# Low parts of both layers' activations: from VectorE to GpSimd

## The chip, the cores and the metric

The kernel runs on one core of a Trainium2 chip. The metric is the device time of one execution in microseconds (us). The core has TensorE (PE, matmuls), VectorE (DVE), ScalarE (ACT), GpSimd (POOL) and SyncE (SP), which here issues the DMAs. Each works through its own queue in order, and they wait for each other by semaphores. TensorE's granted clock was 1.00 of full in nearly every stretch of the profile.

## What is computed

Attention in two stages over packed keys, then two dense layers, all in fp32:

```
x = attention(q, k, v, p)                  # 2304 tokens x 512
h = x @ moe_w_in;  g = softplus(h);  x = g @ moe_w_out      # 512 -> 2048 -> 512
h = x @ moe2_w_in; g = silu(h);      y = g @ moe2_w_out     # 512 -> 2048 -> 512
```

The weights arrive as 64-bit floats.

## The kernel before

Every operand of the large matmuls is kept as two fp32r tiles: a high part, which ScalarE makes by a copy with rounding, and a low part, the operand less its high part, which VectorE makes by a subtraction. A product is then three matmuls: low times high, high times low, high times high.

The **first layer** goes in steps. A unit is a block of 288 tokens (`N0`) and four tiles of 128 hidden features (`GJ`); each step does one tile. `emit_in` (line 484) computes h by 6 matmuls. `emit_out` (line 524) does 12 matmuls of the unit before into a product bank y. `act_scalar` makes the softplus `gt` (line 496, pool of two buffers) and the high part `gh` (line 497) on ScalarE; `act_vector` makes the low part `gl` (line 501). `finish_out` (lines 537 to 541) then adds y to `ya`, which frees the bank. The low part of a unit's last tile is wanted soonest: by the eleventh of the twelve output matmuls in the step right after it. Between these the steps carry out planned items, namely attention (its `ax` is the first layer's input) and the conversion of weights from 64 bits (`wx`, `wraw`, `w` for this layer, `wf`, `whl`, `ohl` for the next). They stand at fixed points of a step; the order on each engine is the order of the code, since the schedule is made by hand.

The **second layer** goes in 24 steps (`step`) of 2 x 384 tokens and 2 x 128 hidden features. It makes a two by two block product of seven products Q1 to Q7 (`products`, line 837) into the banks pA to pD, and sums of them on VectorE (`tu`, `tc`, `c`, by the helper `add`, line 887). Then come silu and high part on ScalarE (lines 907, 908 for g11; 934, 935 for c12; 938, 939 for the pair c2) and three low parts on VectorE into halves of `G` (also through `add`, so the trace gives them line 887). Between the products stand the output tiles of earlier steps (`out_tile`, line 853, 12 matmuls each), and their addition to `ya` (line 866). An even step reads the first token half, also that of the step just before; an odd one reads the second half of two and three steps before. At step 6 the next tokens' operand `xc` is split: high on ScalarE (line 565), low on VectorE (line 569). Its memory was that of the converted weights `whl`, which must first have been stored to `wd`.

GpSimd does a few memsets and the identity matrix at the start, and nothing later.

Of the kernel before, what the change touches and what calls it, by code (L numbers as in the profile page):

```python
# [8 lines left out]
F32 = mybir.dt.float32  # L9
# [4 lines left out]
ALU = mybir.AluOpType  # L14
# [33 lines left out]
def body(ctx, tc, kT, vv, qT, pT, wi1, wo1, wi2, wo2, out):  # L48
    nc = tc.nc
# [130 lines left out]
    def close_stage():  # L180
        stage_stack.close()
        stage_stack.__init__()
# [315 lines left out]
        return gt, gh, gl  # L498

    def act_vector(s, gt, gh, gl):  # L500
        nc.vector.tensor_tensor(out=gl, in0=gt, in1=gh.bitcast(F32), op=ALU.subtract)  # L501
        gs[steps[s]] = gh, gl

    def emit_out(s):
# [223 lines left out]
    def run_steps(end):  # L728
        for s in range(end):
# [21 lines left out]
            if r:  # L751
                act_vector(s, *r)
# [19 lines left out]
    def load_i1(t):  # L772
        if t < NSLOT and (2 * t + 1) // NQ % NJ not in stored:
            held.append(t)
        elif t < NSLOT:
            w = ring_i[t] = wp.tile([P, 2 * DM], F32R, name="w", tag=f"i{t % RI}")
            c = t % (NJ * NQ // 2) * 2 * DM
            nc.sync.dma_start(out=w.bitcast(F32), in_=wd[:, c:c + 2 * DM])
# [39 lines left out]
    def second():  # L818
        psa_stack.close()
        pb = pool("pb", 1, space=PSUM)  # L820
        tmp = st["tmp"]
        slots = [*range(6)]
        G = None
        gs1, frees = {}, {}
        count, put_off = [0], []

        def bank():
            count[0] += 1
            return ps.tile([P, 512], F32, name="y", tag="hy"[count[0] % 2])[:, :N1]

        def products(k, q, out, start):
            p = k * NQ + q
            w = ring_i[p // 2][:, p % 2 * DM:p % 2 * DM + DM]
            x = xcs[k // NJ % 2]
            mm = [(w[:, i * NW + kt * P:i * NW + (kt + 1) * P], x[:, q, h, kt]) for i, h in ((1, 0), (0, 1), (0, 0)) for kt in range(2)]
            for i, (a, b) in enumerate(mm):
                nc.tensor.matmul(  # L837
                    out, lhsT=a, rhs=b, start=start and not i, stop=not start and i == len(mm) - 1,
                    skip_group_check=True,
                )  # L840
            if p % 2:
                load_i1(p // 2 + RI)

        def out_tile(f, t, dm):
            y = bank()
            c = slice(dm * P, (dm + 1) * P)
            for k in 2 * f, 2 * f + 1:
                g = gs1[k, t]
                for j in range(2):
                    w = ring_o[2 * k + j]  # L850
                    wh, wl = w[:, :DM], w[:, DM:]
                    for m, (a, h) in enumerate(((wl, 0), (wh, 1), (wh, 0))):
                        nc.tensor.matmul(  # L853
                            y, lhsT=a[:, c], rhs=G[:, g, h, j], start=(k % 2 == j == m == 0),
                            stop=(k % 2 == j == 1 and m == 2),
                        )
            return y

        def add_out(f, t, dm, y):
            s, f = divmod(f, NPASS)  # L860
            c = (2 * s + t) * N1
            acc = ya[:, dm, c:c + N1]
            if not f:
                nc.scalar.activation(out=acc, in_=y, func=AF.Copy)
            else:
                nc.vector.tensor_tensor(out=acc, in0=y, in1=acc, op=ALU.add)  # L866
            if f == NPASS - 1:
                nc.sync.dma_start(out=out[dm * P:(dm + 1) * P, c:c + N1], in_=acc)

        def out_of(k, i):  # L870
            if not k:
                (dm, y), = emit_out(NS + i)
                return lambda: finish_out(NS + i, dm, y)
            f, t = divmod(k - 2, 2)
            if f < 0:
                return lambda: None
            y = out_tile(f, t, i)
            return lambda: add_out(f, t, i, y)

        def step(k):  # L880
            nonlocal G
            go = lambda p: [fn() for fn in fills.get((k, p), ())]
            y = {}
            b = {n: pb.tile([P, 512], F32, name=f"p{n}")[:, :N1] for n in "ABCD"}
            t = {n: tmp.tile([P, N1], F32, name=f"t{n}") for n in ("a", "u2", "u3", "g11", "c12")}
            c2 = tmp.tile([P, 2, N1], F32, name="c2")
            add = lambda o, i, j, op=ALU.add: nc.vector.tensor_tensor(out=o, in0=i, in1=j, op=op)  # L887
            late = k in (1, 2)
            go("L")
            products(k, Q1, b["A"], True)  # L890
            nc.scalar.activation(out=t["a"], in_=b["A"], func=AF.Copy)  # L891
            products(k, Q6, b["B"], True)
            add(t["u2"], t["a"], b["B"])
            if put_off:
                put_off.pop()()
            go("A0")
            go("D0")
            if not late:
                y[0] = out_of(k, 0)
            products(k, Q2, b["A"], False)  # L900
            products(k, Q7, b["B"], False)
            if late:
                y[0] = out_of(k, 0)
            if G is None:
                G = big.tile([P, 6, 2, 2, N1], F32R, name="G", tag="A")
            g1 = gs1[k, 0] = slots.pop(0)
            nc.scalar.activation(out=t["g11"], in_=b["A"], func=AF.Silu)  # L907
            nc.scalar.activation(out=G[:, g1, 0, 0], in_=t["g11"], func=AF.Copy)
            if not late:
                y.pop(0)()  # L910
            add(t["u3"], t["a"], b["B"])
            add(G[:, g1, 1, 0], t["g11"], G[:, g1, 0, 0].bitcast(F32), ALU.subtract)
            if late:
                y.pop(0)()
            go("D1")
            go("A1")
            go("M")
            y1 = out_of(k, 1)
            y1()
            products(k, Q5, b["C"], True)  # L920
            add(c2[:, 1], t["u3"], b["C"])
            go("D2")
            y2 = out_of(k, 2)
            y2()
            go("A2")
            if k == 1:
                products(k, Q4, b["D"], True)
                products(k, Q3, b["C"], False)
            else:
                products(k, Q3, b["C"], False)  # L930
                products(k, Q4, b["D"], True)
            def first_half():
                add(t["c12"], t["u2"], b["C"])
                nc.scalar.activation(out=t["c12"], in_=t["c12"], func=AF.Silu)  # L934
                nc.scalar.activation(out=G[:, g1, 0, 1], in_=t["c12"], func=AF.Copy)

            def second_half():
                nc.scalar.activation(out=c2, in_=c2, func=AF.Silu)
                nc.scalar.activation(out=G[:, g2, 0], in_=c2, func=AF.Copy)
                add(G[:, g2, 1], c2, G[:, g2, 0].bitcast(F32), ALU.subtract)  # L940

            if k == 1:
                add(c2[:, 0], t["u3"], b["D"], ALU.subtract)
                first_half()
            else:
                first_half()
                add(c2[:, 0], t["u3"], b["D"], ALU.subtract)
            add(G[:, g1, 1, 1], t["c12"], G[:, g1, 0, 1].bitcast(F32), ALU.subtract)
            y3 = out_of(k, 3)
            go("S")  # L950
            while held and (2 * held[0] + 1) // NQ % NJ in stored:
                load_i1(held.pop(0))
            y3()
            for i in frees.pop(k, ()):
                slots.append(i)
            g2 = gs1[k, 1] = slots.pop(0)
            if k == 1:
                put_off.append(second_half)
            else:
                second_half()  # L960
            go("A3")
            go("D3")
            for i, g in (0, g1), (1, g2):
                frees.setdefault(k // 2 * 2 + 2 + i, []).append(g)
            m = (k + 1) // 2 * GJ + (2 - k % 2 * 2)
            for i in range(2):
                if GJ <= m + i < NSUP * NF:
                    load_o1(m + i)
            if k == 0:
                l0_stack.close()  # L970
                open_stage(1, side="right", reuse_waits="tile")

        plan_second()
        for k in range(NSTEP):
            if k == 6:
                close_stage()
                open_xc(1, side="right", reuse_waits="tile")
            step(k)
        for k in NSTEP, NSTEP + 1:
            for i in range(KT):  # L980
                out_of(k, i)()
# [56 lines left out]
```

## Time and profile before

| | us |
|---|---|
| median of 3 runs | 757.52 |
| range of the runs | 756.37 to 760.15 |
| the profiled execution | 756.34 |
| its span (first to last instruction) | 754.6 |
| TensorE busy in it | 745.1 |
| VectorE busy | 494.3 |
| ScalarE busy | 364.7 |
| GpSimd busy | 0.7 |

The busy time of TensorE is modelled at its ends: matmuls overlap, so a row's length (0.29 us for 288 columns) is longer than the distance to the next (0.13 us). What TensorE loses to a wait is read from the distance of starts. "Idle before" is the time in which an engine had nothing to do, with what ended it. Idle time of an engine that TensorE does not wait for costs nothing.

### The profile page before, as it was taken

How to read it: one execution, taken by the hardware profiler on the slowest of the kernel's cores; microseconds unless marked ns; L12 is line 12 of the kernel's file. 1: busy time of each engine (PE TensorE's matmuls, PEld its weight loads, DVE VectorE, ACT ScalarE, POOL GpSimd, SP SyncE). 2: the span in 40 equal slices, each digit the busy share in tenths (PEclk: the TensorE clock that was granted, in tenths of full speed). 3: DMA queues.
4: the chain of work that ended last, by engine and by line, in shares of the span. 5: the costliest groups of instructions: out<-in, count | busy, mean ns of one | idle time of the engine just before them, and what ended most of it. 6: DMA issues, size and time to landing. Idle time of an engine off the chain costs nothing.

```text
span 754.6 us, 13458 instructions
## 1 busy us (share of the span) xinstructions
PE 745.1 (99%) x5488; PEld 713.3 (95%) x5488; DVE 494.3 (66%) x921; ACT 364.7 (48%) x684; POOL 0.7 (0%) x6
## 2 busy tenths in 40 slices
PE   8999999999999999999999999999999999999998
PEld 7777889999999999999999999999999999999998
DVE  3888887879877997897557775743343764334442
ACT  4677786656555565665445553422333323332230
POOL 0000000000000000000000000000000000000000
PEclk9999999999999999999999999999999999999999
DMA  9955032146444452566268888666565557655602
GB/s 343 342 212 183 2 140 113 56 182 197 185 151 182 140 195 86 201 246 267 62 230 336 345 299 325 229 216 204 174 220 193 167 189 238 231 180 168 223 0 85
DMA packets 38974, 145.92 MB, mean 193 GB/s; under 512 B 4352, under 2 KB 7936, under 8 KB 37376
## 3 DMA queue, kind: packets, MB, share of 16 engines
q1 hardware_dynamic: 38912, 145.06, 54.3%
q8 instruction: 43, 0.70, 0.4%
q14 instruction: 19, 0.16, 0.1%
HBM read 117.25 MB, written 27.79 MB: 192 GB/s over the span
## 4 chain that ended last, share of the span: by engine, by line
PE 89%; ACT 4%; DVE 3%; DMA 3%; issue 1%; SPq 1%; ACTq 0%
PE y L853 25%; PE y L524 24%; PE h L484 12%; PE pC L837 6%; PE pA L837 6%; PE pB L837 6%; PE pD L837 3%; PE psa L450 2%; PE y L517 2%; DMA wd<-whl 1%; DMA wraw<-wo 1%; PE psa L357 1%; ACT L419 0%; PE psa L405 0%; ACT ax L431 0%
## 5 line engine op out<-in xcount | busy, mean ns | idle before, releaser
L853 PE MATMUL y<-G,w 128*128 128x384 f32 x1152 | 213.7, 334 | 0.0
L524 PE MATMUL y<-gh,w 128*128 128x288 f32 x960 | 212.1, 296 | 0.3 <-DVE ya L539 0.2
L853 PEld LDWEIGHTS y<-G,w 128*128 128x128 f32 x1152 | 201.0, 188 | 0.0
L524 PEld LDWEIGHTS y<-gh,w 128*128 128x128 f32 x960 | 160.4, 188 | 13.0 <-issue 5.5
L524 PE MATMUL y<-gl,w 128*128 128x288 f32 x480 | 141.8, 295 | 0.1
L484 PE MATMUL h<-ax,vw 128*128 128x288 f32 x768 | 125.0, 298 | 0.3 <-DVE ax L433 0.3
L484 PEld LDWEIGHTS h<-ax,vw 128*128 128x128 f32 x768 | 109.3, 188 | 2.4 <-DVE ax L433 0.5
L524 PEld LDWEIGHTS y<-gl,w 128*128 128x128 f32 x480 | 90.2, 188 | 0.5 <-DVE gl L501 0.5
L866 DVE TENSOR_TENSOR ya<-y,ya 128x384 f32<-128x384 f32 x72 | 40.1, 557 | 64.9 <-PE y L853 64.6
L496 ACT ACTIVATE gt<-h 128x288 f32<-128x288 f32 x120 | 48.6, 405 | 68.6 <-PE h L484 63.9
L501 DVE TENSOR_TENSOR gl<-gt,gh 128x288 fp32r<-128x288 f32 x120 | 54.2, 452 | 25.1 <-ACT gh L497 24.3
L934 ACT ACTIVATE tc<-tc 128x384 f32<-128x384 f32 x24 | 12.6, 526 | 107.0 <-DVE tc L887 107.0
L837 PE MATMUL pC<-xc,w 128*128 128x384 f32 x288 | 57.8, 334 | 0.8 <-DVE c L887 0.8
L887 DVE TENSOR_TENSOR tu<-ta,pB 128x384 f32<-128x384 f32 x48 | 26.5, 552 | 48.4 <-PE pB L837 48.2
L837 PE MATMUL pA<-xc,w 128*128 128x384 f32 x288 | 57.8, 334 | 0.1
L837 PE MATMUL pB<-xc,w 128*128 128x384 f32 x288 | 57.7, 334 | 0.0
L497 ACT ACTIVATE gh<-gt 128x288 fp32r<-128x288 f32 x120 | 53.4, 445 | 3.8
L541 DVE TENSOR_TENSOR ya<-y,ya 128x288 f32<-128x288 f32 x104 | 46.9, 452 | 7.2 <-PE y L524 7.0
L837 PEld LDWEIGHTS pC<-xc,w 128*128 128x128 f32 x288 | 50.5, 188 | 1.1 <-DVE c L887 1.1
L837 PEld LDWEIGHTS pA<-xc,w 128*128 128x128 f32 x288 | 50.5, 188 | 0.4 <-ACT ta L891 0.4
L837 PEld LDWEIGHTS pB<-xc,w 128*128 128x128 f32 x288 | 50.6, 188 | 0.0
L907 ACT ACTIVATE tg<-pA 128x384 f32<-128x384 f32 x24 | 11.8, 491 | 58.2 <-PE pA L837 58.2
(90 smaller groups left out, 793.3 us busy)
## 6 DMA issues: line engine op xcount, KB each, us to landing
w<-wd SPq DMA_DIRECT2D x84, 512.0 KB, 4.0
w<-od SPq DMA_DIRECT2D x48, 512.0 KB, 5.3
wd<-whl SPq DMA_DIRECT2D x8, 1792.0 KB, 7.3
wraw<-wi SPq DMA_DIRECT2D x16, 512.0 KB, 5.5
wraw<-wo SPq DMA_DIRECT2D x16, 512.0 KB, 6.3
raw<-wi SPq DMA_DIRECT2D x16, 512.0 KB, 6.4
raw<-wo SPq DMA_DIRECT2D x16, 512.0 KB, 7.1
od<-ohl SPq DMA_DIRECT2D x16, 512.0 KB, 3.2
```

What stands on the lines that cost most here:

```text
L450: nc.tensor.matmul(t[32 * k:32 * k + 32, r, :512 if wide else 256], lhsT=pts[b][rows, k * NP:(k + 1) * NP], rhs=w[rows, :], start=True, st ...
L484: nc.tensor.matmul(h, lhsT=w, rhs=x, start=(i == 0), stop=(i == len(mm) - 1))
L496: nc.scalar.activation(out=gt, in_=h, func=AF.Softplus)
L497: nc.scalar.activation(out=gh, in_=gt, func=AF.Copy)
L501: nc.vector.tensor_tensor(out=gl, in0=gt, in1=gh.bitcast(F32), op=ALU.subtract)
L517: nc.tensor.matmul(y, lhsT=wo_plain[j][:, c], rhs=gs[u - 1, x], start=(j == js[0]), stop=(j == js[-1]))
L524: nc.tensor.matmul(y, lhsT=w[:, c], rhs=g, start=(j == js[0] and m == 0), stop=(j == js[-1] and m == 2))
L541: nc.vector.tensor_tensor(out=acc, in0=y, in1=acc, op=ALU.add)
L837: nc.tensor.matmul(out, lhsT=a, rhs=b, start=start and not i, stop=not start and i == len(mm) - 1, skip_group_check=True,)
L853: nc.tensor.matmul(y, lhsT=a[:, c], rhs=G[:, g, h, j], start=(k % 2 == j == m == 0), stop=(k % 2 == j == 1 and m == 2),)
L866: nc.vector.tensor_tensor(out=acc, in0=y, in1=acc, op=ALU.add)
L887: add = lambda o, i, j, op=ALU.add: nc.vector.tensor_tensor(out=o, in0=i, in1=j, op=op)
```

## The change

The subtractions that make the low part of the activations are issued to GpSimd. This concerns one line of the first layer (120 instructions of 128x288) and three of the second (24 each, two of 128x384 and one of 128x768). The low parts of weights, of attention's output and of the second layer's input stay on VectorE. So do all sums.

```diff
     def act_vector(s, gt, gh, gl):
-        nc.vector.tensor_tensor(out=gl, in0=gt, in1=gh.bitcast(F32), op=ALU.subtract)
+        nc.gpsimd.tensor_tensor(out=gl, in0=gt, in1=gh.bitcast(F32), op=ALU.subtract)
         gs[steps[s]] = gh, gl
...
             add = lambda o, i, j, op=ALU.add: nc.vector.tensor_tensor(out=o, in0=i, in1=j, op=op)
+            low = lambda o, x, h: nc.gpsimd.tensor_tensor(out=o, in0=x, in1=h.bitcast(F32), op=ALU.subtract)
...
-            add(G[:, g1, 1, 0], t["g11"], G[:, g1, 0, 0].bitcast(F32), ALU.subtract)
+            low(G[:, g1, 1, 0], t["g11"], G[:, g1, 0, 0])
...
-                add(G[:, g2, 1], c2, G[:, g2, 0].bitcast(F32), ALU.subtract)
+                low(G[:, g2, 1], c2, G[:, g2, 0])
...
-            add(G[:, g1, 1, 1], t["c12"], G[:, g1, 0, 1].bitcast(F32), ALU.subtract)
+            low(G[:, g1, 1, 1], t["c12"], G[:, g1, 0, 1])
```

VectorE's queue in the first layer, at the step of 177 us, where a weight tile of `w_out` is converted (lines 148 to 155, and its low part in line 169). Before:

```order
L148 TENSOR_SCALAR wx<-wraw 128x512 [waits DMAHW1_49]
L150 SCALAR_TENSOR_TENSOR wx<-wraw,wx 128x512 [waits DVE_49,Activation_49]
L155 SCALAR_TENSOR_TENSOR wx<-wraw,wx 128x512 [waits DVE_49]
L501 TENSOR_TENSOR gl<-gt,gh 128x288 [waits Activation_49]
L541 TENSOR_TENSOR ya<-y,ya 128x288 [waits PE_49]
L169 TENSOR_TENSOR w<-wx,w 128x512 [waits Activation_49]
L501 TENSOR_TENSOR gl<-gt,gh 128x288 [waits Activation_49]
L541 TENSOR_TENSOR ya<-y,ya 128x288 [waits PE_49]
```

And after, at the same place:

```order
L148 TENSOR_SCALAR wx<-wraw 128x512 [waits DMAHW1_49]
L150 SCALAR_TENSOR_TENSOR wx<-wraw,wx 128x512 [waits DVE_49,Activation_49]
L155 SCALAR_TENSOR_TENSOR wx<-wraw,wx 128x512 [waits DVE_49]
L541 TENSOR_TENSOR ya<-y,ya 128x288 [waits PE_49]
L169 TENSOR_TENSOR w<-wx,w 128x512 [waits Activation_49]
L541 TENSOR_TENSOR ya<-y,ya 128x288 [waits PE_49]
```

Two low parts are gone from this queue, and the additions behind them follow on the conversion. On TensorE the matmul that reads such a low part first waits for GpSimd (`Pool`) where it waited for VectorE, or for nothing of its own, before.

VectorE's queue in the second layer, at step 6 (454 to 466 us), from the sums of the first products to the end of the split of `xc`. Before:

```order
L887 TENSOR_TENSOR tu_5812<-ta,pB 128x384 [waits PE_49]
L887 TENSOR_TENSOR G<-tg_5813,G 128x384 [waits Activation_49]
L569 TENSOR_TENSOR xc_5805<-ya,xc_5805 128x768 [waits DMAHW7_49]
L866 TENSOR_TENSOR ya<-y,ya 128x384 [waits PE_49]
L887 TENSOR_TENSOR c_5815<-tu_5812,pC 128x384 [waits DVE_49,PE_49]
```

After:

```order
L887 TENSOR_TENSOR tu_5812<-ta,pB 128x384 [waits DVE_49,PE_49]
L569 TENSOR_TENSOR xc_5805<-ya,xc_5805 128x768 [waits DMAHW7_49,Activation_49]
L866 TENSOR_TENSOR ya<-y,ya 128x384 [waits PE_49]
L887 TENSOR_TENSOR c_5815<-tu_5812,pC 128x384 [waits DVE_49,PE_49,Pool_49]
```

The low part of `tg` no longer stands ahead of the split. The sum into `c` has a new wait for GpSimd, which reads the former content of `c` in the step before.

## Rows read from the trace of the kernel before

**Rows 1.** The page: span, and busy time, share and instructions by engine.

```profile
span 754.6 us, 13458 instructions
PE 745.1 (99%) x5488; PEld 713.3 (95%) x5488; DVE 494.3 (66%) x921; ACT 364.7 (48%) x684; POOL 0.7 (0%) x6
```

**Rows 2.** Stretches: length, busy us (instructions) by engine, clock, DMA share, GB/s.

```profile
40.00:80.00 40.00, 39.59 (x455) 30.92 (x453) 35.63 (x69) 30.06 (x55) 0.00 (x0) 1.00 0.47 164
80.00:160.00 80.00, 78.84 (x716) 73.93 (x716) 64.36 (x128) 55.17 (x113) 0.00 (x0) 1.00 0.29 108
160.00:240.00 80.00, 79.97 (x632) 75.72 (x632) 66.83 (x134) 47.10 (x99) 0.00 (x0) 1.00 0.46 162
500.00:600.00 100.00, 100.00 (x579) 100.00 (x578) 43.62 (x73) 33.58 (x58) 0.00 (x0) 1.00 0.61 201
```

**Rows 3.** Chain that ended last: start us, us on the chain, what.

```profile
371.11 1.58 PE y L524 x12
...
467.30 2.08 PE y L853 x12
```

**Rows 4.** Groups by line and shape: busy us, mean ns, idle before, releaser.

```profile
L887 DVE TENSOR_TENSOR G<-c,G 128x768 fp32r<-128x768 f32 x24 | 22.8, 952 | 19.3 <-ACT G L939 19.3
...
L887 DVE TENSOR_TENSOR G<-tc,G 128x384 fp32r<-128x384 f32 x24 | 13.4, 558 | 4.2 <-ACT G L935 1.8
...
L887 DVE TENSOR_TENSOR G<-tg,G 128x384 fp32r<-128x384 f32 x24 | 13.2, 551 | 3.0 <-ACT G L908 3.0
```

**Rows 5.** Tile gl: ns min/median/max, first and last start; who waited (us, times).

```profile
L501 DVE TENSOR_TENSOR gl<-gt,gh x120: 416/452/461, 58.5 to 368.4; 128x288 fp32r<-128x288 f32 x120
...
  PEld y L524: 0.9, 3
```

**Rows 6.** Groups by line, GpSimd alone: two of its six instructions.

```profile
masks.py:199 POOL TENSOR_SCALAR_AFFINE_SELECT ident<-ident 128x128 f32<-128x128 f32 x1 | 0.3, 294 | 0.1
...
L1031 POOL MEMSET const-float32-0.0<- 128x1 f32 x1 | 0.1, 99 | 0.2 <-issue 0.2
```

**Rows 7.** Timeline, end of an ordinary unit: start us, us, engine, line, what.

```profile
206.76 0.44 ACT L497 ACTIVATE gh<-gt 128x288 fp32r<-128x288 f32 x1
...
209.81 0.30 PE L524 MATMUL y<-gl,w 128*128 128x288 f32 x1
```

**Rows 8.** Timeline, unit end with a weight conversion before it.

```profile
176.57 0.45 ACT L497 ACTIVATE gh<-gt 128x288 fp32r<-128x288 f32 x1
...
177.57 0.69 DVE L155 SCALAR_TENSOR_TENSOR wx<-wraw,wx 128x512 int32<-128x512 int32 x1
...
178.18 0.45 DVE L501 TENSOR_TENSOR gl<-gt,gh 128x288 fp32r<-128x288 f32 x1
178.23 0.43 PE L524 MATMUL y<-gh,w 128*128 128x288 f32 x2
...
178.69 0.40 PE L524 MATMUL y<-gl,w 128*128 128x288 f32 x1
```

**Rows 9.** Timeline, second layer, step 6.

```profile
459.99 1.58 ACT L565 ACTIVATE xc<-ya 128x768 fp32r<-128x768 f32 x2 [5.72 <-DMA wd<-whl]
...
461.91 2.25 PE L853 MATMUL y<-G,w 128*128 128x384 f32 x12
...
462.54 0.56 DVE L887 TENSOR_TENSOR G<-tg,G 128x384 fp32r<-128x384 f32 x1 [3.00 <-ACT G L908]
463.02 0.95 DVE L569 TENSOR_TENSOR xc<-ya,xc 128x768 fp32r<-128x768 f32 x1
...
464.35 0.55 DVE L887 TENSOR_TENSOR c<-tu,pC 128x384 f32<-128x384 f32 x1
...
464.95 1.31 PE L837 MATMUL pC<-xc,w 128*128 128x384 f32 x6 [0.80 <-DVE c L887]
```

**Rows 10.** Timeline, end of the last step.

```profile
732.34 18.88 PE L853 MATMUL y<-G,w 128*128 128x384 f32 x108
...
732.65 0.53 ACT L935 ACTIVATE G<-tc 128x384 fp32r<-128x384 f32 x1
```

## The prediction

> **What bounds the kernel now.** I read the busy times first [rows 1], then the stretches [rows 2], then what the two sides of the changed lines do, then single moments on the timeline. TensorE is busy 745.1 of 754.6 us [rows 1]; from 160 to 240 us it is busy 79.97 of 80, and from 500 to 600 us all 100 [rows 2]. VectorE is busy 66%, GpSimd 0.7 us in all [rows 1]. So the time is a sum of matmuls, 1.58 us for twelve of 288 columns and 2.08 us for twelve of 384 [rows 3]. The change takes none away. It can gain only where TensorE waits for VectorE, and lose only where TensorE comes to wait for GpSimd, or for a VectorE that GpSimd holds up. The whole idle time of TensorE is 754.6 - 745.1 = 9.5 us, most of it at the start and after the last matmul, where no low part is computed.
>
> **What moves.** 120 subtractions of 128x288 [rows 5] and, in the second layer, 24 + 24 of 128x384 and 24 of 128x768 [rows 4]. VectorE loses 54.2 us (120 x 0.452) and 13.2 + 13.4 + 22.8 = 49.4 us of work, 103.6 us of its 494.3. It also no longer stands still for ScalarE's high part before these lines; 19.3 us of that stood before the widest of them alone [rows 4]. What is queued behind each of them on VectorE comes forward: in the first layer the addition that empties a product bank, in the second the next sums.
>
> **What one costs on GpSimd.** The trace has no GpSimd subtraction; its rows bound the price. From below I take VectorE's own 0.45, 0.55 and 0.95 us [rows 4, 5]. From above: GpSimd's select over 128 elements took 0.294 us and a memset of one element 0.099 us [rows 6], so (294 - 99) / 127 = 1.53 ns an element read once. A subtraction reads two inputs; with each counted in full, 0.10 + 288 x 3.06 ns = 0.98 us, 1.27 us for 384 and 2.45 us for 768. Nothing says which end is nearer, so I take the middle, 0.7, 0.9 and 1.7 us, and keep both ends. [...]
>
> **Are they in time?** First layer: the high part of the last tile of an ordinary unit ends at 206.76 + 0.44 = 207.20 us, and TensorE wants the low part at 209.81 [rows 7]: 2.61 us. Of 30 units 19 have 2.60 to 2.64. The dearest GpSimd price, 0.98, leaves 1.6 us. The tightest place has 177.02 to 178.69 us [rows 8], 1.67 us, some 0.3 less without the stall that is in it: 1.37, and 0.98 still fits. Second layer: the step that has least is the last one, where no further products stand between. ScalarE's high half ends at 732.65 + 0.53 = 733.18 [rows 10]. The long row from 732.34 holds twelve matmuls of the step's own tile, 2.08 us, and the low part is wanted at the eighth of the next, 7 x 0.173 us on: 735.6. That is 2.4 us for 0.55 to 1.27. In earlier even steps two more products, 2.08 us, lie in between, and the 768-wide part is read a step later. So no low part comes late: cost nothing, hidden by the other tiles' matmuls, and 2.6 us is the price from which that ends in an ordinary unit.
>
> **The waits added.** TensorE carries 180 waits for GpSimd in place of some for VectorE. Twelve matmuls of 384 take 2.08 us where some of them wait for weights and ScalarE just as well [rows 3], so a wait that is met costs nothing. ScalarE's next write of gt, tg, tc and c2 waits for GpSimd's reading of the old one; gt has two buffers, and two steps are 5.2 us (119 steps in 368.4 - 58.5 us [rows 5], 2.60 each), against 0.98. VectorE's addition into c2 waits for the 768-wide part of the step before; that starts when the step's last copy is done, and the next addition needs the fifth group of products of the next step; even between the first two steps, which have the fewest matmuls, that is over 4 us, against 2.45. Behind that addition stand on VectorE the x splits and the output additions, none of which is then held. No DMA is issued from GpSimd, so no transfer is moved.
>
> **What goes away.** Twice in the first layer TensorE waits for gl because VectorE does a weight conversion first. At 177.02 the high part is there; VectorE is in the conversion until 178.18, and gl ends at 178.63 [rows 8]. The two matmuls before it take 178.69 - 178.23 = 0.46 us where the pace is 2 x 0.132, and the waiting one 0.40 instead of 0.30: 0.30 us lost. The same pattern stands at 260 us: together 0.6; the 0.9 us of waiting for gl [rows 5] is the upper end, 0 the lower. In the second layer, at 461.91, twelve matmuls start whose successor could begin 2.08 us later, at 463.99; it begins at 464.95 and waits for VectorE's sum c [rows 9]. VectorE stood 3.00 us before the low part of G, which waited for ScalarE, which itself was released at 459.99 by a store. Without that low part the split of x needs only ScalarE's first copy (459.99 + 1.58/2 = 460.8), ends at 461.7, the two additions behind it wait for their products alone and c is done by 462.7. The 0.96 us go, and 0.11 of a slow restart: 1.07. If the split waited for both copies (461.57), c would end at 463.5, still in time.
>
> **Sum.** 0.6 + 1.07 = 1.67 us. The profiled execution took 756.34 us: its span of 754.6 and 1.7 around it; that would become 754.7. It lies 1.2 us below the median of 757.52, and from the median the forecast is 757.5 - 1.7 = 755.8 us.
>
> **Rival 1, collisions.** GpSimd has run beside nothing in this trace [rows 6], so what VectorE loses when both work on the same memory is unbounded by rows. The place is 58 to 160 us, where VectorE is busiest: 35.63 of 40, then 64.36 of 80 us [rows 2]. If each GpSimd subtraction (0.98) holds up one VectorE instruction for its whole length, VectorE nets 0.98 - 0.45 = +0.53 us a step. From 58.5 to 80 us are 8 steps, 4.2 us, against 21.5/40 x 4.37 = 2.3 us of free time: 1.9 us late. From 80 to 160 us are 31 steps, 16.4 against 15.6: 0.8. Together 2.7 us, so 755.8 + 2.7 = 758.5 us. It costs from a hold-up above 0.45 us on. From 160 us on VectorE has 80 - 66.83 = 13 us free in 80 [rows 2] and no attention chain waits for it, so I let the loss end there. [...]
>
> **Rival 2, more relief.** TensorE idles 40 - 39.59 = 0.41 and 80 - 78.84 = 1.16 us in those same stretches [rows 2]. If an earlier VectorE ends all of it: 755.8 - 1.6 = 754.2 us.
>
> **Rival 3, slower: GpSimd becomes the bound.** From 2.60 us a subtraction on, the steps' own pace [rows 5], GpSimd paces the first layer. At 2.75 us, 119 x 0.15 = 18 us are added to 757.5 and nothing is gained: 775 us. It speaks against this that 2.6 is 2.7 times my upper price.
>
> **That it does nothing:** if both waits only move to GpSimd or to ScalarE, 757.5 us.
>
> **Chances.** Forecast 0.56, collisions 0.20, more relief 0.12, nothing 0.08, GpSimd the bound 0.04. About 0.5%, 3.8 us, is what a measurement of this kernel can tell from no change. The forecast, "nothing" and nearly all of the collisions lie inside 753.7 to 761.3; of more relief a third may measure beyond. Faster 0.05, within 0.89, slower 0.06. The three runs before spread 756.37 to 760.15, so 753.0 to 760.0 holds the forecast, more relief and collisions with this spread, and leaves out the slow case and the ends.
>
> **What would show it.** Right: GpSimd near 155 us busy (120 x 0.7 + 48 x 0.9 + 24 x 1.7 = 168; 125 to 237 by the ends), VectorE some 100 us less, no wait of TensorE for GpSimd, the stalls at 178, 260 and 464 gone, TensorE's busy share unchanged. Collisions show as VectorE rows of two inputs that are longer than before, and as new TensorE idle time between 58 and 160 us. TensorE waits for gl or G from GpSimd would prove the timing step wrong; a span below 752 us would say that the matmuls' own pace had slack that I did not see.

## The result, and the profile after

The changed kernel is slower: median 766.21 us (765.65 to 767.82) against 758.84 us for the kernel before on the same chip; over all runs that is a ratio of 1.0104 with a 95% interval of 1.0068 to 1.0139. I had forecast 755.8 us and a range of 753.0 to 760.0. The profiled execution's span is 764.5 us in place of 754.6, so 9.9 us are to be found. The two medians are only 7.4 us apart: the profiled execution of the kernel before (756.34 us) lies 2.5 us below its median, that of the changed kernel (766.26) at its own.

The page of the changed kernel, the lines that answer to [rows 1]:

```profile
span 764.5 us, 13747 instructions
...
PE 748.6 (98%) x5488; PEld 714.1 (93%) x5488; DVE 443.6 (58%) x729; ACT 363.4 (48%) x684; POOL 209.4 (27%) x198
```

VectorE is 50.7 us less busy, not 103.6: about half of what was taken from it came back. GpSimd is busy for 209 us (I had 168; the ends of my prices give 103 and 237, and the 125 of the prediction was a wrong sum). The stretches that answer to [rows 2], with the same columns:

```profile
80.00:160.00 80.00, 78.78 (x718) 73.96 (x717) 57.85 (x99) 55.64 (x113) 27.07 (x29) 1.00 0.29 107
160.00:240.00 80.00, 77.92 (x608) 72.62 (x606) 61.99 (x101) 45.11 (x96) 30.07 (x30) 1.00 0.42 150
240.00:320.00 80.00, 77.91 (x607) 72.61 (x606) 59.89 (x97) 44.58 (x96) 29.29 (x30) 1.00 0.47 162
...
500.00:600.00 100.00, 100.00 (x579) 100.00 (x578) 31.55 (x53) 31.84 (x55) 24.27 (x19) 1.00 0.61 196
```

From 80 to 160 us, where I had placed the collisions, TensorE lost nothing (78.78 against 78.84). From 160 to 240 us, where it had been busy for 79.97 of 80, it now issues 608 instructions in place of 632. In the second layer it is as full as it was. The start of the second layer shows it in one number. Tile pA, first and last start, before:

```profile
L837 PE MATMUL pA<-xc,w x288: 334/334/443, 368.9 to 723.8; 128*128 128x384 f32 x144
```

and after:

```profile
L837 PE MATMUL pA<-xc,w x288: 334/334/443, 378.1 to 733.8; 128*128 128x384 f32 x144
```

The first layer ends 9.2 us later, and that is nearly all of the 9.9. What TensorE waited for in the changed kernel (in total, times, longest):

```profile
PE y L524 <- DVE ya L541: 2.2, 5, 1.1
PE y L524 <- POOL gl L501: 1.9, 3, 0.8
PE pC L837 <- DVE c L887: 1.4, 1, 1.4
...
PE h L484 <- DVE vw L462: 1.4, 2, 0.7
```

In the kernel before TensorE's groups show (busy us, mean ns, idle before, releaser):

```profile
L524 PE MATMUL y<-gh,w 128*128 128x288 f32 x960 | 212.1, 296 | 0.3 <-DVE ya L539 0.2
...
L837 PE MATMUL pC<-xc,w 128*128 128x384 f32 x288 | 57.8, 334 | 0.8 <-DVE c L887 0.8
```

Four of the five large names are new or larger, and three of these four are VectorE's own instructions, in lines that the change did not edit. By the distance of starts (a matmul's row, 0.30 us, is 0.17 longer than the 0.13 to the next start, and hides as much of each wait) the new gaps between 178 and 351 us add up to 9 us at eleven places.

What GpSimd needed, by line and shape (busy us, mean ns | idle before, releaser), answering to the price I had bounded from [rows 4 to 6]:

```profile
L501 POOL TENSOR_TENSOR gl<-gt,gh 128x288 fp32r<-128x288 f32 x120 | 115.4, 962 | 262.0 <-ACT gh L497 189.3 <-PE y L524 37.4 <-PE h L484 18.7
L888 POOL TENSOR_TENSOR G<-c,G 128x768 fp32r<-128x768 f32 x24 | 44.4, 1848 | 27.9 <-ACT G L940 14.9 <-PE pB L837 7.5 <-PE y L853 4.3
...
L888 POOL TENSOR_TENSOR G<-tc,G 128x384 fp32r<-128x384 f32 x24 | 24.4, 1016 | 159.0 <-ACT G L936 159.0
```

And tile gl, ns min/median/max: 

```profile
L501 POOL TENSOR_TENSOR gl<-gt,gh x120: 804/821/1630, 58.8 to 377.8; 128x288 fp32r<-128x288 f32 x120
```

An undisturbed one takes 0.82 us, inside my bounds of 0.45 to 0.98; the mean is 0.96, since some last up to twice as long. The place of [rows 8], in the timeline of the changed kernel, shows why:

```profile
174.32 0.44 ACT L497 ACTIVATE gh<-gt 128x288 fp32r<-128x288 f32 x1
...
174.78 0.69 DVE L199 SCALAR_TENSOR_TENSOR wx<-raw,wx 128x512 int32<-128x512 int32 x1
174.90 1.24 POOL L501 TENSOR_TENSOR gl<-gt,gh 128x288 fp32r<-128x288 f32 x1 [0.51 <-ACT gh L497]
...
175.50 1.19 DVE L203 SCALAR_TENSOR_TENSOR wx<-raw,wx 128x512 int32<-128x512 int32 x1
...
176.73 0.63 ACT L244 ACTIVATE ohl<-wx 128x512 fp32r<-128x512 f32 x1 [1.96 <-DVE wx L203]
177.26 0.67 ACT L138 ACTIVATE wraw<-wraw 128x512 f32<-128x512 f32 x1
...
177.83 0.40 ACT L496 ACTIVATE gt<-h 128x288 f32<-128x288 f32 x1
...
178.25 0.45 ACT L497 ACTIVATE gh<-gt 128x288 fp32r<-128x288 f32 x1
...
178.83 1.05 POOL L501 TENSOR_TENSOR gl<-gt,gh 128x288 fp32r<-128x288 f32 x1 [2.69 <-ACT gh L497]
...
179.93 0.41 PE L524 MATMUL y<-gl,w 128*128 128x288 f32 x1 [0.78 <-POOL gl L501]
```

GpSimd's subtraction begins at 174.90 while VectorE is in a conversion, and lasts 1.24 us, 0.42 more than 0.82. The next conversion begins at 175.50 while GpSimd works, and lasts 1.19 us in place of 0.69. By these lengths the two take turns: the subtraction has 0.67 us left when the first conversion ends at 175.47, and the second conversion has 0.55 us left when the subtraction ends at 176.14. ScalarE has to copy that conversion's result before it comes to the next tile: it stands for 1.96 us (1.41 in the kernel before), and its gt and gh come late behind it. The high part ends at 178.70. TensorE would have wanted the low part at about 178.64, before the high part was even there.

### The profile page after: what moved, and what is told of

Its sections match the earlier page's. It is cut to its first block, busy times and chain, and to the rows that moved or that the text cites. A ratio compares the mean times of both kernels' runs of the same rounds, so it can differ in the third digit from the quotient of the medians.

```text
span 764.5 us, 13747 instructions
## 1 busy us (share of the span) xinstructions
PE 748.6 (98%) x5488; PEld 714.1 (93%) x5488; DVE 443.6 (58%) x729; ACT 363.4 (48%) x684; POOL 209.4 (27%) x198
## 4 chain that ended last, share of the span: by engine, by line
PE 74%; DVE 12%; ACT 6%; DMA 5%; issue 2%; SPq 1%; DVEq 0%; POOL 0%; ACTq 0%; POOLq 0%
PE y L853 24%; PE y L524 16%; PE h L484 8%; PE pC L837 6%; PE pA L837 6%; PE pB L837 6%; DMA wd<-whl 3%; PE pD L837 3%; PE psa L450 2%; DVE wx L203 2%; PE y L517 2%; DVE wx L199 1%; DMA wraw<-wo 1%; DVE vw L462 1%; DVE wx L150 1%
## 5 line engine op out<-in xcount | busy, mean ns | idle before, releaser
L501 POOL TENSOR_TENSOR gl<-gt,gh 128x288 fp32r<-128x288 f32 x120 | 115.4, 962 | 262.0 <-ACT gh L497 189.3
L888 POOL TENSOR_TENSOR G<-tc,G 128x384 fp32r<-128x384 f32 x24 | 24.4, 1016 | 159.0 <-ACT G L936 159.0
L888 POOL TENSOR_TENSOR G<-c,G 128x768 fp32r<-128x768 f32 x24 | 44.4, 1848 | 27.9 <-ACT G L940 14.9
```

The source lines that it names most:

```text
L501: nc.gpsimd.tensor_tensor(out=gl, in0=gt, in1=gh.bitcast(F32), op=ALU.subtract)
L888: low = lambda o, x, h: nc.gpsimd.tensor_tensor(out=o, in0=x, in1=h.bitcast(F32), op=ALU.subtract)
```

## Experiments

Three theories. **C (collision)**: GpSimd's subtraction and VectorE's instructions beside it hold each other up, and what stands behind them makes TensorE wait. **L (late)**: the subtraction is simply slower on GpSimd and arrives late where there was little slack. **2**: the loss is in the second layer. The column on the right is the first start of pA in each kernel's profile, that is, how much later the first layer ended than the 368.9 us of the kernel before. It is one execution each: l2_only, whose first layer is untouched, shows 0.6 us by chance.

| kernel | ratio to before | 95% interval | first layer ends later by, us |
|---|---|---|---|
| changed kernel | 1.0104 | 1.0068 to 1.0139 | 9.2 |
| l1_only | 1.0117 | 1.0090 to 1.0143 | 9.2 |
| l2_only | 0.9978 | 0.9962 to 0.9993 | 0.6 |
| dummy_sub | 1.0264 | 1.0232 to 1.0297 | 20.6 |
| l1_free | 1.0008 | 0.9988 to 1.0027 | 0.2 |
| l1_conv | 1.0116 | 1.0100 to 1.0131 | 8.3 |
| relax_after | 1.0042 | 1.0026 to 1.0059 | 5.0 |
| relax_before | 0.9986 | 0.9968 to 1.0005 | -0.1 |
| relax_l2 | 0.9971 | 0.9958 to 0.9984 | 0.3 |
| l1free_l2 | 0.9982 | 0.9969 to 0.9995 | 0.1 |
| dummy_copy | 1.0039 | 1.0021 to 1.0057 | 2.5 |
| dummy_memset | 1.0038 | 1.0022 to 1.0054 | 1.9 |

**Which layer: l1_only and l2_only.** The changed kernel with one of its two parts undone:

```diff
-            low = lambda o, x, h: nc.gpsimd.tensor_tensor(...)      # l1_only
+            low = lambda o, x, h: nc.vector.tensor_tensor(...)
...
-        nc.gpsimd.tensor_tensor(out=gl, in0=gt, ...)                # l2_only
+        nc.vector.tensor_tensor(out=gl, in0=gt, ...)
```

> Only the first layer's gl goes to GpSimd, the second layer's low parts stay on VectorE. Theory C (collisions): a GpSimd subtraction holds up a VectorE weight conversion that starts beside it by about 0.5 us (in the changed kernel one of 0.69 us takes 1.19), ScalarE waits in order for the conversion and the next gh comes late; the new stalls of TensorE between 178 and 350 us add up to about 9 us, so this kernel keeps nearly all of the loss: 764 to 766 us, ratio about 1.009. Theory L (GpSimd's gl takes 0.82 us in place of 0.45 and is late by itself): 0.4 us at each of the two or three tight places, 1 us, ratio about 1.001. Theory 2 (the loss sits in the second layer): no change.

> Only the second layer's three low parts go to GpSimd, gl stays on VectorE. Theory C: few VectorE instructions of two SBUF inputs stand beside them, all in the steps that still convert weights; TensorE's one stall there, 0.96 us before at 464 us, lies between 0 and 1.6 us: ratio 0.999 to 1.001. My prediction's own step for this layer: the stall goes, 1.1 us less. Theory 2: the whole loss, ratio 1.01.

The first layer alone has the whole loss. The second layer alone gains 0.2% (1.7 us by the ratio, 0.5 to 2.9 by its interval), against the 1.1 us I had for it. Theory 2 falls. The two together, 9.2 us lost in the first layer and 1.7 gained in the second, fit the 7.4 us between the medians. In l2_only the place of [rows 9] reads:

```profile
462.54 2.25 PE L853 MATMUL y<-G,w 128*128 128x384 f32 x12
...
464.30 0.55 DVE L887 TENSOR_TENSOR c<-tu,pC 128x384 f32<-128x384 f32 x1
...
464.90 1.31 PE L837 MATMUL pC<-xc,w 128*128 128x384 f32 x6
```

The twelve matmuls end at 462.54 + 2.08 = 464.62, and the next begins at 464.90, 0.28 us later in place of 0.96.

**Collision or lateness: dummy_sub.** The kernel before, with a subtraction on GpSimd beside gl whose result nobody reads:

```diff
...
         nc.vector.tensor_tensor(out=gl, in0=gt, in1=gh.bitcast(F32), op=ALU.subtract)
+        nc.gpsimd.tensor_tensor(out=scr, in0=gt, in1=gh.bitcast(F32), op=ALU.subtract)
```

> The kernel before, with gl still on VectorE, and beside it the same subtraction on GpSimd into a scratch tile that nobody reads; only ScalarE's next write of gt waits for it. Theory C: VectorE is held up as in the changed kernel and besides keeps its 54 us of gl, so the loss is at least as large: 765 us or more, ratio 1.010 to 1.025, and conversion rows of 1.0 to 1.2 us stand in the trace. Theory L: no TensorE instruction waits for GpSimd, so no loss: ratio 1.000.

The largest loss of all, 2.6%, a little above what C gave. TensorE's new large waits have the name of VectorE alone:

```profile
PE y L526 <- DVE ya L543: 5.7, 8, 1.5
PE y L526 <- DVE gl L502: 5.1, 4, 1.7
```

So a GpSimd that no TensorE instruction waits for costs TensorE 20.6 us in the first layer. Two things are in it that the changed kernel does not have: gl, itself with two inputs, stays on VectorE and is held up too (up to 1.06 us in place of 0.45), and after a wait of 1.7 us that ended at 272.3 us TensorE's granted clock fell for a while to 0.50 of full, which cost 1.5 us. One way remains by which GpSimd could be late here: ScalarE's write of gt waits until GpSimd has read what the buffer held two steps before, and 16 of ScalarE's waits have its name. But that reading had always ended at least 0.43 us before the write began (0.50 in the changed kernel), so it held nothing up. L falls as the cause. It need not be without any share in the changed kernel, where 1.9 us of TensorE's waits do have the name of GpSimd's gl.

**With what it collides: l1_free and l1_conv.** gl goes to GpSimd in half of the steps, by whether a weight conversion is planned there:

```diff
...
+        eng = nc.vector if s in conv_at else nc.gpsimd      # l1_free; the other way round in l1_conv
-        nc.vector.tensor_tensor(out=gl, in0=gt, ...)
+        eng.tensor_tensor(out=gl, in0=gt, ...)
```

> gl goes to GpSimd only in the 60 steps in which no weight conversion is planned, and stays on VectorE in the 60 others; second layer as before. Theory C: most of the collisions with conversions are gone, and with them most of the loss: ratio 0.998 to 1.003. Theory L: the tight places (at 178 and 260 us before) are steps with a conversion, so also about none. A theory by which it is the mere count of GpSimd subtractions: half of the loss, ratio 1.005.

> The complement of l1_free: gl goes to GpSimd only in the 60 steps in which a weight conversion is planned, and stays on VectorE in the 60 others; second layer as before. If the loss is made by GpSimd's subtractions beside the conversions, these 60 carry all of what 120 carry in l1_only: ratio 1.008 to 1.012. If it is made by the number of subtractions, half: 1.005. If it takes both kinds of steps together (a delay that builds up from step to step), less than half.

Sixty subtractions beside conversions carry nearly the whole loss (8.3 of the 9.2 us in the first layer), sixty others none. It is the company, not the number. In l1_conv TensorE waits between 150 and 390 us for the same three names as in the changed kernel:

```profile
PE y L527 <- DVE ya L544: 1.7, 3, 1.1
PE y L527 <- POOL gl L504: 1.6, 2, 0.8
PE h L486 <- DVE vw L464: 1.4, 2, 0.7
```

**What in GpSimd holds VectorE up: dummy_copy and dummy_memset.** As dummy_sub, but GpSimd reads one tile, or (but for one column) only writes:

```diff
...
+        nc.gpsimd.tensor_copy(scr, gh.bitcast(F32))                          # dummy_copy
...
+        nc.gpsimd.tensor_copy(scr[:, :1], gh.bitcast(F32)[:, :1])            # dummy_memset
+        for i in range(2):
+            nc.gpsimd.memset(scr2[i], 0.0)
```

> As dummy_sub, but GpSimd only copies gh (128x288, one input) into the scratch tile, from the same moment, and nobody reads it. If GpSimd holds up VectorE whenever it reads this memory, conversions are held up by the length of the copy, shorter than the 0.82 us of a subtraction: a loss, but smaller than dummy_sub's 2.6%: ratio 1.004 to 1.018. If it takes GpSimd's two inputs: 1.000.

> As dummy_sub, but beside each gl GpSimd copies one column and then fills two scratch tiles of 128x296 with zeros: it is busy for some 0.7 us from the same moment on, and only writes. If what VectorE and GpSimd exclude each other from is reading, the conversions of two inputs (0.69 us) keep their length and the loss is small: ratio 0.999 to 1.005. If any access of GpSimd holds VectorE up, about dummy_sub's loss: 1.015 to 1.026.

Both times came out at 1.004, which does not tell the two apart (for dummy_copy it is the low end of what I had expected). The lengths of VectorE's conversions (ns min/median/max) decide. The kernel before, a conversion of two inputs:

```profile
L203 DVE SCALAR_TENSOR_TENSOR wx<-raw,wx x16: 691/693/695, 166.9 to 337.2; 128x512 int32<-128x512 int32 x16
```

The changed kernel, with a conversion of one input beside it:

```profile
L197 DVE TENSOR_SCALAR wx<-raw x32: 409/457/1391, 135.2 to 452.5; 128x512 int32<-128x512 int32 x32
...
L203 DVE SCALAR_TENSOR_TENSOR wx<-raw,wx x16: 692/1188/1191, 167.1 to 346.7; 128x512 int32<-128x512 int32 x16
```

dummy_copy, the same conversion of two inputs:

```profile
L204 DVE SCALAR_TENSOR_TENSOR wx<-raw,wx x16: 691/794/800, 167.2 to 340.3; 128x512 int32<-128x512 int32 x16
```

dummy_memset, both:

```profile
L199 DVE TENSOR_SCALAR wx<-raw x32: 413/419/965, 136.0 to 443.6; 128x512 int32<-128x512 int32 x32
...
L205 DVE SCALAR_TENSOR_TENSOR wx<-raw,wx x16: 691/692/694, 167.2 to 339.3; 128x512 int32<-128x512 int32 x16
```

And the addition of the changed kernel that has one input in PSUM and one in SBUF, 104 of them:

```profile
L541 DVE TENSOR_TENSOR ya<-y,ya x104: 419/450/458, 51.8 to 391.9; 128x288 f32<-128x288 f32 x104
```

A GpSimd that only writes leaves the two-input conversion at 0.69 us in all 16 cases (13 of them run beside it); one that reads a tile stretches it to 0.80, one that subtracts to 1.19. The one-input conversion of 0.42 us is stretched even by the memsets, to 0.60 to 0.73 where they alone run beside it, and to 0.97 where the one-column copy does too. The addition that takes one input from PSUM keeps its length (median 0.45 us in both kernels, none above 0.46), though 60 of the 104 run beside a subtraction. Why memsets stretch the conversion of one input and not that of two was not shown.

In time, the first layer lost 2.5 and 1.9 us, which is most of the 0.4%. What the two profiled executions lost beyond that stands mainly at the place of [rows 9], at which relax_before, with no subtraction on GpSimd, waits as long:

```profile
PE pC L837 <- DVE c L887: 2.7, 1, 2.7
```

Behind this wait the granted clock fell to 0.50 in all three (in dummy_copy from 470.19 to 473.60 us), which cost dummy_copy another 1.6 us: its twelve matmuls into pC and pD took 3.75 us from start to start there, those of l2_only 2.19. In the kernel before, whose wait there was 0.8 us, it stayed at 1.00.

**By which way it reaches TensorE: relax_after, relax_before and relax_l2.** ScalarE's copy of a converted weight of w_out goes one step later, so that it no longer stands ahead of gt and gh in the step of the conversion; VectorE's low part of that weight moves back with it:

```diff
...
-        yield "A2"
+        yield "A0"        # of the next step
         high_o(n, 2)
-        yield "D0"
+        yield "D1"
         low_o(n)
```

(and so in `conv_w`). It is made to the changed kernel, the kernel before and l2_only.

> The changed kernel with one thing moved: the high part of a converted weight of w_out is copied by ScalarE one step later (point A0 of the next step in place of A2 of the same), and its low part follows at D1. VectorE's conversions are held up as before, but ScalarE has no conversion of the same step to wait for, ahead of the next gt and gh. If the loss comes by ScalarE's place in the queue (conversion late, so gh late, so gl late), most of it goes: 757 to 760 us, ratio 1.000 to 1.003. If TensorE waits for VectorE's own late instructions (the addition that empties y, the low part of vw), at least half stays: 1.005 or more.

> The kernel before, with ScalarE's copy of a converted weight of w_out one step later, and no GpSimd in it: the control of relax_after. No effect of its own: 0.998 to 1.001. Then relax_after's gain on the changed kernel (1.0104 to 1.0042) is the way by ScalarE's queue alone. If it is itself faster by 0.6%, that gain had nothing to do with GpSimd.

> l2_only with the same later copy on ScalarE: gl stays on VectorE, the second layer's low parts go to GpSimd. It is the control of relax_after and the candidate for a faster kernel: the two waits for gl at 178 and 260 us (0.3 us each) come from a conversion ahead of gl on VectorE, which stays, but gh comes earlier there. 755 to 757 us, ratio 0.996 to 0.999. If the later copy costs by itself (a weight late), above 1.000.

Of the 1.04% that the change costs, 0.62 go, though VectorE is held up as much as before; of the 9.2 us in the first layer 4.2. By the same instruction's median in the kernel before, VectorE's instructions of the first layer from 55 us on are stretched by 25.1 us in all in relax_after, and by 25.9 in the changed kernel. The conversions of two inputs for the second layer's w_out:

```profile
L203 DVE SCALAR_TENSOR_TENSOR wx<-raw,wx x16: 691/1045/1193, 167.6 to 342.5; 128x512 int32<-128x512 int32 x16
```

The control moves by 0.1%, and its interval holds 1. So about half of the loss takes the way by ScalarE's queue. That the rest comes by VectorE's own was not tried by itself; it is read from TensorE's largest wait that is left, for the additions that empty y:

```profile
L524 PE MATMUL y<-gh,w 128*128 128x288 f32 x960 | 212.9, 297 | 2.4 <-DVE ya L541 2.0
```

Neither of my two figures was right; with two ways that each carry about half, neither could be. ScalarE's waits for the conversions (in total, times, longest), in the kernel before:

```profile
ACT ohl L244 <- DVE wx L203: 20.4, 16, 1.5
...
ACT w L167 <- DVE wx L155: 8.7, 11, 1.3
```

and in the changed kernel:

```profile
ACT ohl L244 <- DVE wx L203: 30.5, 16, 2.8
...
ACT w L167 <- DVE wx L155: 12.7, 12, 1.8
```

relax_l2 is the fastest kernel of the study, 756.39 us, 0.29% below the kernel before. Of the two waits for gl the one at 178 us is gone; the one at 260 us stands as before. The interval leaves out 1, but the gain is within the 0.5% that I called no change.

**The rest: l1free_l2.** The changed kernel, with gl left on VectorE in steps with a conversion.

> The changed kernel, but in the 60 steps with a planned weight conversion gl stays on VectorE: 60 gl and all of the second layer on GpSimd. Theory C: no loss, and what l2_only gained is kept: 755 to 758 us, ratio 0.997 to 1.001. If the second layer's collisions matter too, above 1.002.

As C said. Together with l2_only it shows that the second layer's collisions are real but cost no more than its change gains: the sums of x, 128x768 from two SBUF inputs, take 1.52 us in place of 0.95 in the changed kernel, and none of TensorE's waits there has their name.

## Why the prediction was wrong

**What bounds the kernel** was right: TensorE's sum of matmuls is unchanged, and the loss is waiting.

**The price on GpSimd** was right within its bounds: 0.82, 1.02 and 1.85 us undisturbed, where I took 0.7, 0.9 and 1.7. The middle was 8 to 15% low. From my own prices the low end of GpSimd's busy time should have read 103 us (120 x 0.45 + 48 x 0.55 + 24 x 0.95) and not 125; nothing else rests on it.

**"Are they in time?" failed.** I measured the slack from the end of the high part, with that end held fixed, and it would have been enough: the low part at 178.83 lasts 1.05 us, not 1.4. But the high part itself came late, by 1.4 us against TensorE's pace at the tightest place. It hangs on VectorE by ScalarE's in-order queue: conversion, copy of its result, then gt and gh. In the kernel before this chain showed as ScalarE's wait for the conversion (1.27 us in the step of [rows 8]), and I had not drawn it. "No low part comes late" was false at 178, 263 and 350 us.

**Rival 1 named the mechanism (a VectorE that GpSimd holds up), and its place and size were wrong.** That a subtraction would hold up one instruction for its whole length, 0.98 us, was my assumption; the runs showed 0.4 us on average. The first of its signs came: VectorE's conversions of two inputs took up to 1.19 us in place of 0.69 (L203, `wx`). That it would be rows of two inputs no row had shown, and the conversion of one input was stretched as well, from 0.42 to up to 1.39 us (L197). I looked for the place where VectorE is busiest, gave the loss 2.7 us, and let it end at 160 us with the words that VectorE has 13 us free in 80. The loss of the first layer was 9.2 us, and 9.1 of it came between 178 and 351 us. VectorE's free time does not protect a chain: at a collision one VectorE instruction ends those 0.4 us later, and in steps that follow each other with a conversion in each, the delay passes on through ScalarE. From 80 to 160 us twelve conversions were held up, by 4.2 us in all, and TensorE lost nothing; from 160 to 200 us thirteen, by 6.0 us, and TensorE lost 2.7. There conversions stand closer (28 in 40 us, against 35 in 80). The row that I should have started from is the number of VectorE's weight conversions beside gl, and who waits for them, not VectorE's busy share. The mechanism had 0.20, and the chance of slower by over 0.5% 0.06; that was far too little for a resource whose sharing no row of the trace showed.

**What goes away.** The 0.6 us at 178 and 260 us did not come: each grew from 0.3 to 1.4 us. The 1.07 us at [rows 9] came in l2_only for the most part (0.28 us are left), and not in the changed kernel (1.4 us of waiting). The step was right that the split of x no longer stands behind the low part. It was wrong to hold fixed the moment at which a store of converted weights releases ScalarE: counted from the end of the first layer that store began 1.7 us later and took 12.05 us in place of 10.88. The changed kernel's chain (start, us, what):

```profile
459.97 12.05 DMA wd<-whl
...
472.04 0.86 ACT xc L565
```

and before:

```profile
449.10 10.88 DMA wd<-whl
459.99 1.58 ACT xc L565 x2
```

This wait varies from profile to profile: 0 to 1.7 us in the five kernels with the second layer's low parts on GpSimd, 0.8 to 3.2 us in the eight with them on VectorE, and the 0.8 is the kernel before. Its store of 10.88 us is the shortest of the thirteen (11.5 to 13.0 in the others), so the row from which I priced this step was the mildest case. By the means, 2.3 and 0.9 us, an estimate of what the change gains here is 1.4 us. Why the store takes longer in one than in another was not tried and stays open.

**The waits added** cost nothing, as forecast: where no conversion is near, the new waits for GpSimd leave no gap (l1_free: no wait of TensorE for GpSimd's gl, and a first layer that ends 0.2 us later).

## What to carry to other kernels

An operation moved to an idle engine is not free if it holds up a busy one, as GpSimd's subtractions did here with VectorE's conversions (0.69 us became 1.19, and the first layer ended 9.2 us later): count the neighbour's instructions that run beside it, and follow who waits for each, through every in-order queue. Slack measured from an event that itself hangs on the neighbour is no slack. If the work must move, move it first where the neighbour's instructions keep their length, as those with one input in PSUM did here (most of the second layer's: 0.55 to 0.56 us in both kernels; l2_only gained 0.2%), and leave it where they grow and something waits for them, as the conversions did.

## What the runs showed of the hardware

- Beside each other, VectorE's conversions of 0.69 us took up to 1.19 (L203, `wx`) and GpSimd's subtractions of 0.82 up to 1.63 in the changed kernel. Memsets on GpSimd, which only write, stretched the conversions of one input from 0.42 to up to 0.73 us in dummy_memset, and left those of two inputs at 0.69.
- One column copied on GpSimd took 0.41 us on average in dummy_memset, a memset of 296 columns 0.34.
- Behind a single wait of TensorE of 1.7 to 3.1 us the granted clock fell for a while to 0.50 in five of the thirteen profiles (l1_only, dummy_sub, relax_before, dummy_copy, dummy_memset), each time at a cost of 1.5 to 1.6 us. Behind waits as long, of 1.8 us in l1_free and 3.2 in l1_conv, it stayed at 1.00.
